# Retention, experts and a Fourier mixing block on one core: batch 0's stores and batch 1's loads ahead of the first layer, another order of conversions, folds, splits and rows

## The chip, the core and the metric

The kernel runs on one core of one Trainium2 chip. The metric is the device time of one execution in microseconds (us). The kernel before takes 799.32 us, the median of three runs (796.78, 799.32, 805.36).

## What is computed

Three blocks follow each other, on 4 batches of S = 576 rows of D = 512 numbers. The change lies in the third.

```python
x = attention(q, k, v)            # retention, 8 heads of 64
x = moe(x)                        # one of 8 experts for each row, F = 1024
X = np.real(np.fft.fft(np.fft.fft(x, axis=1), axis=2))
u = x + X
un = (u - mean(u)) / sqrt(var(u) + 1e-6)
return u + np.maximum(un @ w_ch1, 0) @ w_ch2     # 512 -> 2048 -> 512
```

## The kernel before

Products are made in 16-bit floats: each matrix is split into a high part (a scaled cast on ScalarE, L281) and a low part (what the cast lost, on VectorE, L286), and a product is three matrix products (high by high, high by low, low by high).

**The third block.** `channels` (L1577 and after) computes it. `tr` is the object that transforms a batch. Of one batch `load` (L1224) brings the rows in three tiles; `even` and `odd` (L1243, L1257) fold a tile on VectorE, with the tiles `fee` and `foo` as results, and `twice` (L1267) folds tiles 0 and 1 once more; `down` (L1279) multiplies the folded tiles by tables of cosines and sines, five groups to a batch; `take` copies a group's result out on ScalarE; `across` multiplies these by the second table, and `merge` adds the result to the rows; `sums` and `rate` make mean and rate of each row; `norm` writes the normalized rows as high and low part to the DRAM tensor `un`, and `keep` writes u to the DRAM tensor `u`. `steps(b)` is a generator that does all this for one batch in pieces.

**Batch 0.** Its 576 rows are transformed while TensorE ends the last expert. The rows of the first 512 then go through the first layer, in 16 steps f of 128 of the 2048 columns. `first(f, ...)` (L1651) issues the 12 products of 128 by 512 of a step; the first four steps are issued ahead of the loop. In the loop `for f in range(16)` ScalarE makes the relu (`gr`, L1852) and its cast (`hd`, L1853), and VectorE the low part of `hd` (L1854). Between these steps the loop calls generators, one piece at a time: `last` (the end of batch 0's norms and the stores `keep`), `rest` (splits of the first layer's pieces 4 to 7; conversion of pieces 6 and 7 of the second layer's matrix from 64-bit floats, `raw` to `wst`; their `absmax` on ScalarE; the peak over all pieces, with a product on TensorE, `peak`; `scale`, whose last instruction makes `ws`; the splits of pieces 6 and 7 and then of 0 to 5, two to a step), and from f = 7 on `tr.steps(1)` (batch 1's load, folds and transform).

**The second layer.** `for t in range(4)` makes the output of 128 rows in one pass over 16 rows of the matrix, one for each f: three products of 128 by 512 each (L1870), all added in one bank. Row f needs `hd` of step f, and the piece f // 2 of the second layer's matrix. Between the rows stand the rest of `tr.steps(1)` and pieces of `sums` (which add up blocks of the matrix, for the next loop). After the third pass `fetch(512)` asks for the next rows of `un`, transposed, in `gxt`. The loop over r0 = 512 and on takes 256 rows at a time and is the same in both kernels; j counts its turns.

**Useless products.** `still(n, ps)` (L1618) issues n products of 128 by 512 whose result nobody reads: STILL[0] = 8 ahead of batch 0's first `down`, STILL[1] = 22 in batch 1's first `down`, STILL[2] = 16 ahead of the first product of row 512.

**What sets the order.** Each engine works through its instructions in the order in which the program issues them; that order is the order of the calls. All loads and stores on SyncE (the DMA queue SPq) too go in the order of their calls. Pools set when a buffer comes free: three banks `g1` for the first layer, three buffers `gr`.

Of the kernel before, what the change touches and what calls it, by code (L numbers as in the profile page):

```python
# [20 lines left out]
E, FF = 8, 2048  # L21
# [22 lines left out]
EARLY_C1 = 2  # L44
LATE = 4
IDLE = 2, 2, 9, 7, 0
STILL = 8, 22, 16


PEAKS = 10, 14  # L50
# [2 lines left out]
DONE = 14  # L53
# [958 lines left out]
def moe(octx, tc, nc, A, xs, x2, rows_in, rows_out, pieces, weights, who, conv, low, start, beyond, z, padded, hid0, mt0, wst, small):  # L1012
# [126 lines left out]
    for e in range(E):  # L1139
        w, n = weights(e), CAPS[e] if e < E - 1 else HEAD  # L1140
        if e == E - 1:
            pieces.more = None
        xt, mt = X.pop(e)
        tiles = (n + 127) // 128

        todo = halves(weights, conv, 2 * e, 8, [("fetch", (fetch, e + 1))] if e + 1 < E else ()) if e else first
        hid = wk.tile([128, 2, 8, n], FP16, tag="hid", name="hid", padded_shape=[128, 2, 8, CAP])
        hid = [hid[:, x] for x in range(2)]
        for f in range(8):
            if e == 0 and f == 0:  # L1150
                four = [bank()[:, 0:n] for _ in range(4)]
                for part in (0, 2, 1):
                    for g in range(4):
                        products(nc, four[g], *w.dst, xt, f + g, (part,))
            if e == 0 and f < 4:
                ps = four[f]
            else:
                ps = bank()[:, 0:n]
                products(nc, ps, *w.dst, xt, f)
            for do in todo[f]:  # L1160
                do()
            if f == 4 and e + 2 < E:
                pad(e + 2)
            for _ in relu(nc, ps, hid, f):
                pass
        fs, fill = factors(w, mt, tiles + (end.n + 127) // 128, small) if e == E - 1 else factors(w, mt, tiles)
        if e == E - 1:
            end.fs = fs

        def sides(mt=mt, tiles=tiles, n=n, e=e):  # L1170
            for i, m in ((n // 128, n % 128), (tiles + end.n // 128, end.n % 128 if e == E - 1 else 0)):
                if m:

                    to, k = mt[:, i, 0:1], 128 // m
                    nc.vector.tensor_scalar(out=to, in0=to, scalar1=float(k), scalar2=side[k], op0=ALU.mult, op1=ALU.add)

        late = 0 < e < E - 1
        if not late:
            fill()
            sides()  # L1180
        if e == E - 1:
            mx.close()
            yield
        todo = halves(weights, conv, 2 * e + 1, tiles, [("factors", (f,)) for f in (fill, sides) if late]) if e else [[sizes]]
        for t in range(tiles):

            amid = partial(weights(e + 1).spread, 0, lambda: bank()[:, 0:128]) if e and t == 0 else None
            out(w, hid, mt, fs, t, n, todo[t], amid)
    end.hidden(range(LATE), bank)
    ctx.close()  # L1190
    yield end
# [12 lines left out]
class Transform:  # L1204
# [16 lines left out]
        nc.vector.memset(self.eps, 1e-6)  # L1221
        self.xy, self.ee, self.oo, self.z, self.st = {}, {}, {}, {}, {}

    def load(self, b, places=None):  # L1224

        nc, x2, r = self.nc, self.x2, b * S
        self.xy[b], self.ee[b], self.oo[b], self.z[b] = xy, ee, oo, z = places or self.own
        nc.gpsimd.memset(xy[0][0:1, 1, :], 0.0)
        nc.gpsimd.memset(xy[1][0:1, 1, :], 0.0)
        for t in range(3):  # L1230
            nc.gpsimd.memset(oo[t][:, 0:1], 0.0)
        for t, (k, n) in enumerate(TL):
            m = n if t < 2 else 2 * n
            i = nc.sync.dma_start(out=xy[t][:m, 0, :], in_=x2[r + k : r + k + m, :])
            if b < 2 and t == 0:
                self.rows.before(i)
            p = 1 if t < 2 else 0
            by_rows(nc, xy[t][p:n, 1, :], x2[r + k + n : r + k + 2 * n - p, :])
# [306 lines left out]
    def steps(self, b, wait=0):  # L1545

        self.load(b)
        yield
        for t in range(3):
            self.even(b, t)  # L1550
            if wait:
                yield
            self.odd(b, t)
            yield
        self.twice(b, 0)
        self.twice(b, 1)
        yield
        for _ in range(wait):
            yield
        for i in range(5):  # L1560
            self.take(b, i, self.down(b, i))
            yield
        for t in range(3):
            if t:
                self.sums(b, t - 1)
            self.merge(b, t, *self.across(b, t))
            yield
        self.sums(b, 2)
        yield
        yield from self.end(b)  # L1570


def channels(ctx, tc, nc, A, w1, w2, un, u, out, tr, wst, idn, late, jobs):
# [17 lines left out]
    def fetch(r):  # L1591
        X[r] = xt = room().rearrange("p (k n) -> p k n", k=8)
        nc.sync.dma_start_transpose(out=xt, in_=un[r : r + 256, :])  # L1593
# [11 lines left out]
        q, tag = ((p1, "g1"), (tr.ps, "z"), (tr.ps, "z"), (tr.ps, "z"), (p1, "g1"), (p1, "g1"), (p2, "g2"), (p2, "g2"))[turn[0] % 8]  # L1605
        return q.tile([128, 512], FP32, tag=tag, name="bank")

    late.hidden(range(LATE, 8), bank)
    tr.root()
    tr.turn(idn)  # L1610
    for j in range(EARLY_C1, 4):
# [10 lines left out]

    tr.still = still
    still(STILL[0], z[0])
    tr.even(0, 0)
    leave()
    tr.even(0, 1)
    tr.twice(0, 0)
# [57 lines left out]
    turns = {i: tr.turned(0, i, norms[i], xt, bank()) for i in (0, 3)}  # L1686
    weave(adds[2])
    leave()
    next(turns[0])
    next(turns[3])  # L1690
    next(rates[1])
# [16 lines left out]
    for f in range(4):  # L1708
        first(f, place(f, 1), half[1])

    def last():

        tr.norm(0, 2, 2)
        tr.sums(0, 2)
        yield
        weave(tr.rate(0, [2]))
        tr.norm(0, 5)
        yield
        for i in range(6):
            tr.keep(0, i)  # L1720
        yield

    def convert(j):

        V = nc.vector
        t = w2.pieces[j] = wst.tile([128, 1024], FP32, tag="wst", name="wst")
        for i in range(2):
            raw = wst.tile([128, 512, 2], I32, tag="wst", name="raw")
            nc.sync.dma_start(out=raw, in_=jobs[8 + j][0][:, i])
            convert_first(V, raw, t[:, 512 * i : 512 * i + 512].bitcast(I32))  # L1730
            yield
            convert_second(V, raw, t[:, 512 * i : 512 * i + 512].bitcast(I32))
            yield
        w2.absmax(j)

    def rest():

        for j in range(4, 8):
            w1.split(j)
            yield  # L1740
        done = DONE - 8
        for j in range(done, 8):
            yield from convert(j)
        for j in range(done, 8):
            nc.sync.dma_start(out=jobs[8 + j][1], in_=w2.pieces[j])
        w2.peak(0)
        for j in range(2):
            w2.load(j)
        yield
        w2.spread(0)  # L1750
        w2.scale(0)
        for j in range(done, 8):
            w2.split(j)
        yield
        for j in range(2, done):
            w2.load(j)
        for j in range(done):
            w2.split(j)
            if j % 2:
                yield  # L1760


    def blocks(k):
# [21 lines left out]
    def sums():  # L1785
# [31 lines left out]
    TWICE = 1, 4  # L1817
    WAIT = 1
    LEFT = 6
    T_SLOTS = [(t, f) for t in range(0, 4) for f in (4, 12)]  # L1820

    def old(r, n):

# [12 lines left out]
        )  # L1836


    more, left, hid, end = tr.steps(1), rest(), [], last()
    for f in range(16):  # L1840
        if f < 4:
            ps = ahead[f]
        else:
            ps = p1.tile([128, 512], FP32, tag="g1", name="g1")
            first(f, ps, xt)
        if f >= 7:
            next(more, None)
        next(end, None)
        next(left, None)
        r = wk.tile([128, 512], FP32, tag="gr", name="gr")  # L1850
        hd = hp.tile([128, 2, 512], FP16, tag="hd", name="hd")
# [11 lines left out]
        V.tensor_scalar(out=fs[:, j : j + 1], in0=fs[:, 0:1], scalar1=c, scalar2=None, op0=ALU.mult)  # L1863
    us = [old(256 * a, 256) for a in range(2)]
    left = sums()
    for t in range(4):
        ps = p2.tile([128, 512], FP32, tag="g2", name="g2")
        for f in range(16):
            for i, (m, x) in enumerate(((h2, 0), (h2, 1), (l2, 0))):
                nc.tensor.matmul(  # L1870
                    out=ps,
                    lhsT=hid[f][:, x, 128 * t : 128 * t + 128],
                    rhs=m[:, f // 2, 512 * (f % 2) : 512 * (f % 2) + 512],
                    start=(f == 0 and i == 0),
                    stop=(f == 15 and i == 2),
                )
            if f == 7 or (t, f) == (0, 3):
                next(more, None)
            if (t, f) in T_SLOTS:
                next(left, None)  # L1880
        next(more, None)
        if t == 2:
            for _ in more:
                pass
            fetch(512)
# [478 lines left out]
```

## Time and profile before

| | us |
|---|---|
| median of three runs | 799.32 |
| the profiled execution | 797.81 |
| its span in the trace | 796.0 |
| TensorE busy in it | 736.8 (93%) |
| VectorE busy in it | 591.1 (74%) |
| ScalarE busy in it | 411.5 (52%) |

The profile is of one execution. PE is TensorE, DVE VectorE, ACT ScalarE, SP SyncE; times count from the span's start. A busy share over the whole span is a mean over stages with different limits, so the stages are read one by one. PEclk is the granted clock of TensorE as a share of full speed: 1.00 is 2.4 GHz, 0.50 is 1.2 GHz. A line of a timeline has the start, the time until the end of the last of its instructions, the engine, the line of the kernel, what it writes and reads, and in brackets how long the engine was idle before it, and what released it.

### The profile page before, as it was taken

How to read it: one execution, taken by the hardware profiler on the slowest of the kernel's cores; microseconds unless marked ns; L12 is line 12 of the kernel's file. 1: busy time of each engine (PE TensorE's matmuls, PEld its weight loads, DVE VectorE, ACT ScalarE, POOL GpSimd, SP SyncE). 2: the span in 40 equal slices, each digit the busy share in tenths (PEclk: the TensorE clock that was granted, in tenths of full speed). 3: DMA queues.
4: the chain of work that ended last, by engine and by line, in shares of the span. 5: the costliest groups of instructions: out<-in, count | busy, mean ns of one | idle time of the engine just before them, and what ended most of it. 6: DMA issues, size and time to landing. Idle time of an engine off the chain costs nothing. (4 is left out here: it accounts for less than half of the span.)

```text
span 796.0 us, 17230 instructions
## 1 busy us (share of the span) xinstructions
PE 736.8 (93%) x6571; PEld 549.3 (69%) x6571; DVE 591.1 (74%) x1432; ACT 411.5 (52%) x829; POOL 128.6 (16%) x225
## 2 busy tenths in 40 slices
PE   8888797999999989889989999899899999999996
PEld 5677684646556646557644547778788888888885
DVE  3678887599888987867796976968867595736462
ACT  1356656479798887845827544416432361414140
POOL 3566443002201220113000011010010101010101
PEclk9999999999999998999998999999999999999998
DMA  9998349999999999950538257610370016110000
GB/s 296 360 301 298 130 130 303 322 284 379 273 341 327 271 309 330 254 181 29 168 95 314 96 185 200 181 54 2 123 192 2 27 61 168 52 53 3 28 1 27
DMA packets 91930, 142.29 MB, mean 179 GB/s; under 512 B 48116, under 2 KB 49017, under 8 KB 90814
## 3 DMA queue, kind: packets, MB, share of 16 engines
q1 hardware_dynamic: 87246, 126.78, 50.5%
q0 software_dynamic: 4592, 14.31, 5.0%
q8 instruction: 54, 0.88, 0.4%
q14 instruction: 38, 0.31, 0.1%
HBM read 97.55 MB, written 35.12 MB: 167 GB/s over the span
## 5 line engine op out<-in xcount | busy, mean ns | idle before, releaser
L1656 PE MATMUL g<-gxt,wh 128*128 128x256 f16 (+1 forms) x992 | 143.3, 284 | 2.4 <-DMA gxt<-un 2.4
L1970 PEld LDWEIGHTS <-hd 128*128 128x128 f16 x1176 | 115.1, 98 | 26.3 <-issue 6.0
L1656 PEld LDWEIGHTS <-wh 128*128 128x128 f16 x1056 | 103.2, 98 | 28.3 <-issue 7.1
L286 DVE SCALAR_TENSOR_TENSOR wl<-wst,ws,wh 128x1024 f16<-128x1024 f32 (+1 forms) x82 | 100.4, 1253 | 9.6 <-ACT wh L281 9.4
L281 ACT ACTIVATE wh<-wst,ws 128x1024 f16<-128x1024 f32 x80 | 89.2, 1141 | 29.2 <-DVE ws L274 29.2
L815 PE MATMUL ps<-xt,wh 128*128 128x320 f16 (+4 forms) x544 | 80.1, 287 | 13.0 <-DMA xt<-xs 7.9
L845 PE MATMUL ps<-wh,hid 128*128 128x512 f16 (+2 forms) x528 | 84.5, 302 | 0.2 <-ACT hid L831 0.2
L815 PEld LDWEIGHTS <-wh 128*128 128x128 f16 x640 | 58.0, 101 | 38.0 <-issue 19.8
L1830 POOL DMA_INDIRECT out<-u,orow x18 | 19.3, 1075 | 389.7 <-DVE u L1999 291.3
L1970 PE MATMUL g<-wh,hd 128*128 128x256 f16 x448 | 78.3, 273 | 2.5 <-DVE s L1941 1.6
L1656 PE MATMUL g<-gxt,wl 128*128 128x256 f16 (+1 forms) x496 | 80.4, 285 | 0.0
L845 PEld LDWEIGHTS <-hid 128*128 128x128 f16 (+2 forms) x792 | 46.4, 100 | 42.3 <-issue 2.7
L1941 DVE SCALAR_TENSOR_TENSOR s<-g,r 128x256 f32<-128x256 f32 x168 | 53.1, 371 | 29.6 <-ACT hd L1935 28.9
L239 ACT ACTIVATE wh<-wst 128x1024 bf16<-128x1024 f32 x66 | 69.3, 1051 | 4.9 <-DVE wst L311 3.8
L1999 DVE SCALAR_TENSOR_TENSOR u<-g,ffs,u 128x256 f32<-128x256 f32 (+1 forms) x63 | 34.1, 567 | 49.3 <-PE g L1970 48.7
L1934 ACT ACTIVATE r<-g 128x256 f32<-128x256 f32 x56 | 21.1, 378 | 90.9 <-PE g L1656 84.9
L1970 PE MATMUL g<-e,hd 128*128 128x256 f16 x504 | 61.6, 277 | 5.5 <-DVE u L1999 4.5
L1914 ACT ACTIVATE hd<-s 128x640 f16<-128x640 f32 x56 | 41.3, 737 | 47.1 <-DVE s L1941 47.0
L859 POOL DMA_INDIRECT x<-y,mt x25 | 32.1, 1285 | 194.7 <-ACT y L857 156.3
L1970 PE MATMUL g<-wl,hd 128*128 128x256 f16 x224 | 61.0, 272 | 0.0
L1656 PEld LDWEIGHTS <-wl 128*128 128x128 f16 x528 | 51.9, 98 | 11.7 <-issue 1.1
L845 PE MATMUL ps<-wl,hid 128*128 128x512 f16 (+2 forms) x264 | 56.3, 301 | 0.0
(302 smaller groups left out, 1292.5 us busy)
## 6 DMA issues: line engine op xcount, KB each, us to landing
wst<-in_moe_w SPq DMA_DIRECT2D x64, 512.0 KB
raw<-in_ch SPq DMA_DIRECT2D x14, 1024.0 KB
qk<-in_qkv SPq DMA_DIRECT2D x18, 512.0 KB
vk<-in_qkv SPq DMA_DIRECT2D x16, 512.0 KB
pair<-ch SPq DMA_DIRECT2D x32, 256.0 KB
ch<-d SPq DMA_DIRECT2D x14, 512.0 KB
wst<-ch SPq DMA_DIRECT2D x14, 512.0 KB
u<-u SPq DMA_DIRECT2D x9, 512.0 KB
```

The lines of the kernel that those rows point to most:

```text
L239: self.nc.scalar.activation(out=x, in_=t, func=ACTF.Abs, accum_out=self.am[:, j : j + 1])
L281: self.nc.scalar.activation(out=self.dst[0][:, j, :], in_=self.pieces[j], func=ACTF.Copy, scale=self.by(j))
L286: self.nc.vector.scalar_tensor_tensor(out=l[:, j, c], in0=self.pieces[j][:, c], scalar=self.by(j), in1=h[:, j, c], op0=ALU.mult, op1=ALU.s ...
L815: nc.tensor.matmul(out=ps, lhsT=m[:, k, 128 * f : 128 * f + 128], rhs=xt[:, x + k, :], start=(k == 0 and i == 0), stop=(k == 3 and i == last),
L845: nc.tensor.matmul(out=ps[r * j : r * j + r, 0:d], lhsT=hid[x][:, f, 128 * t : 128 * t + r], rhs=m[:, 4 + f // 2, c : c + d], start=(f == ...
L859: nc.gpsimd.indirect_dma_start(out=x2[:, :].rearrange("t (k d) -> (t k) d", k=k), out_offset=bass.IndirectOffsetOnAxis(ap=mt, axis=0), in_ ...
L1656: nc.tensor.matmul(out=ps, lhsT=m[:, k + 4 * (f // 8), 128 * (f % 8) : 128 * (f % 8) + 128], rhs=xt[x][:, k, :], start=(k == 0 and i == 0) ...
L1914: nc.scalar.activation(out=hd[:, 0, 2:7], in_=s, func=ACTF.Copy, scale=C2 / 2)
L1934: nc.scalar.activation(out=r, in_=p[:, 1:3], func=ACTF.Relu)
L1941: V.scalar_tensor_tensor(out=d, in0=x, scalar=0.0, in1=y, op0=ALU.max, op1=op)
L1970: nc.tensor.matmul(out=ps, lhsT=hid[k][:, y, x, :], rhs=E[w][m][k], start=(k == 0 and m == y == 0), stop=(k == 7 and y == 1),)
L1999: V.scalar_tensor_tensor(out=y, in0=p, scalar=fs[:, c : c + 1], in1=y, op0=ALU.mult, op1=ALU.add)
```

## The change

1. STILL becomes 0, 0, 4.
2. In the last expert, the last two splits of its list are issued after the last output tile and no more inside it.
3. Batch 0's first fold is issued among the last expert's tiles.
4. Batch 0's stores `keep` of tiles 0 and 1, the loads of piece 6 (`begin(6)`) and of batch 1's tiles 0 and 1 are issued ahead of the first layer.
5. One generator `beside` takes the place of `rest` and `last`: batch 1's folds (f2, f6, f7, f8) come ahead of the conversions (f9 to f12), the peak is at f13, the scale and the splits of pieces 6 and 7 at f14, the splits of pieces 0 to 5 at f15, all six in one step.
6. Batch 1's transform (`across_rows`) starts at f = 10 with one `down` a step; the rest of it and the pieces of `sums` have new places in the second layer (MORE, T_SLOTS), and `fetch(512)` comes after the fourth row of the third pass.
7. The second layer takes its rows in the order 12 to 15, 0 to 11.

```diff
-STILL = 8, 22, 16
+STILL = 0, 0, 4
...
-            out(w, hid, mt, fs, t, n, todo[t], amid)
+            do = todo[t] if e < E - 1 else todo[t][:-1]
+            out(w, hid, mt, fs, t, n, do, amid)
+        if e == E - 1:
+            todo[-1][-1]()
...
-    late.hidden(range(LATE, 8), bank)
+    late.hidden(range(LATE, LATE + 1), bank)
+    tr.even(0, 0)
+    late.hidden(range(LATE + 1, 8), bank)
...
     still(STILL[0], z[0])
-    tr.even(0, 0)
     leave()
...
+    for i in (0, 3, 1, 4):
+        tr.keep(0, i)
...
+    begin(DONE - 8)
...
+    tr.load(1, (0, 1))
...
+    def beside():
+        done = DONE - 8
...
         tr.norm(0, 2, 2)
         tr.sums(0, 2)
+        w1.split(4)
         yield
         weave(tr.rate(0, [2]))
         tr.norm(0, 5)
+        for i in (2, 5):
             tr.keep(0, i)
+        tr.load(1, (2,))
+        yield
+        tr.even(1, 0)
+        w1.high(5)
+        tr.odd(1, 0)
+        yield
+        w1.low(5)
+        yield
+        w1.split(6)
+        begin(7)
+        yield
+        w1.split(7)
+        yield
+        tr.even(1, 1)
+        tr.odd(1, 1)
+        yield
+        tr.even(1, 2)
+        tr.odd(1, 2)
+        yield
+        tr.twice(1, 0)
+        tr.twice(1, 1)
+        yield
         for j in range(done, 8):
+            for _ in convert(j):
+                yield
+        for j in range(2):
+            w2.load(j)
         for j in range(done, 8):
             nc.sync.dma_start(out=jobs[8 + j][1], in_=w2.pieces[j])
         w2.peak(0)
-        for j in range(2):
-            w2.load(j)
         yield
         w2.spread(0)
         w2.scale(0)
...
         for j in range(done):
             w2.split(j)
-            if j % 2:
-                yield
...
+    DOWNS = 10
+    MORE = [(0, 3), (0, 7), (0, 15), (1, 3), (1, 7), (1, 9), (1, 11), (1, 13), (1, 15), (2, 1), (2, 3)]
+    T_SLOTS = [(1, 14), (2, 6), (2, 9), (2, 12), (2, 15), (3, 3), (3, 8), (3, 13)]
+    ROWS = *range(12, 16), *range(12)
...
-        if f >= 7:
+        next(left, None)
+        if f >= DOWNS:
             next(more, None)
-        next(end, None)
-        next(left, None)
...
-        for f in range(16):
+        for at, f in enumerate(ROWS):
...
-                    start=(f == 0 and i == 0),
-                    stop=(f == 15 and i == 2),
+                    start=(at == 0 and i == 0),
+                    stop=(at == 15 and i == 2),
```

The order of ScalarE's instructions at the end of the first layer, before. L281 are the highs of the second layer's splits; the last `gr` and `hd` are those of f = 15, the two ahead of them of f = 14.

```order
L1852 ACTIVATE gr_7291<-g1_7260 128x512
L1853 CAST hd_7292<-gr_7291 128x512
L1306 COPY fz3_6316<-zps_7309 128x256
L1306 COPY fz3_6316<-zps_7309 128x34
L281 ACTIVATE wh1_77<-wst_7279,ws_7213 128x1024
L281 ACTIVATE wh1_77<-wst_7281,ws_7213 128x1024
L1852 ACTIVATE gr_7319<-g1_7296 128x512
L1853 CAST hd_7320<-gr_7319 128x512
L281 ACTIVATE wh1_77<-wst_7283,ws_7213 128x1024
L281 ACTIVATE wh1_77<-wst_7285,ws_7213 128x1024
```

The same place in the change (L1890 and L1891 are the relu and the cast; the first row is f = 14's cast):

```order
L1891 CAST hd_7262<-gr_7261 128x512
L281 ACTIVATE wh1_77<-wst_7208,ws_7217 128x1024
L281 ACTIVATE wh1_77<-wst_7210,ws_7217 128x1024
L281 ACTIVATE wh1_77<-wst_7279,ws_7217 128x1024
L281 ACTIVATE wh1_77<-wst_7281,ws_7217 128x1024
L281 ACTIVATE wh1_77<-wst_7283,ws_7217 128x1024
L281 ACTIVATE wh1_77<-wst_7285,ws_7217 128x1024
L1457 COPY bs_7315<-zps_7299 128x256
L1458 COPY sm_7313<-zps_7300 128x1
L1459 COPY df_7314<-zps_7300 128x1
L1890 ACTIVATE gr_7327<-g1_7266 128x512
L1891 CAST hd_7328<-gr_7327 128x512
```

Six highs and three copies of batch 1's merge now stand between the cast of f = 14 and the relu of f = 15; before, two highs stood there and two copies.

VectorE's order around the end of the first layer's step f = 15, in the change: the last of the six lows (L286), batch 1's first merge, and the low part of f = 15's `hd` (`hd_7328`).

```order
L286 SCALAR_TENSOR_TENSOR wl1_78<-wst_7285,ws_7217,wh1_77 128x1024
L1441 MEMSET mv_7307 128x6
L1442 MEMSET sq_7308 128x6
L1460 TENSOR_TENSOR sm_7313<-zps_7300,bs_7315 128x256
L1461 TENSOR_TENSOR df_7314<-zps_7300,bs_7315 128x256
L1464 TENSOR_TENSOR fxy0_6302<-fxy0_6302,sm_7313 128x257
L1465 TENSOR_TENSOR fxy0_6302<-fxy0_6302,df_7314 128x255
L1464 TENSOR_TENSOR fxy0_6302<-fxy0_6302,df_7314 128x257
L1465 TENSOR_TENSOR fxy0_6302<-fxy0_6302,sm_7313 128x255
L1466 BN_STATS st_7306<-fxy0_6302 128x6
L1467 BN_AGGR mv_7307<-st_7306 128x2
L1892 TENSOR_TENSOR hd_7328<-gr_7327,hd_7328 128x512
```

Before, the merge stood behind all `hd`, and two lows stood between one `hd` and the next.

TensorE's order at the start of the second layer, before (the last group of `down`, then rows f = 0 and 1; `hd_6894` is f = 0's):

```order
L1291 MATMUL zps_7309<-f_sn_1971,foo2_6311 128x290
L1870 LDWEIGHTS hd_6894
L1870 MATMUL g2_7335<-wh1_77,hd_6894 128x512
L1870 LDWEIGHTS hd_6894
L1870 MATMUL g2_7335<-wh1_77,hd_6894 128x512
L1870 LDWEIGHTS hd_6894
L1870 MATMUL g2_7335<-wl1_78,hd_6894 128x512
```

And in the change, the end of the third row and the fourth (`hd_7328` is f = 15's):

```order
L1909 MATMUL g2_7351<-wl1_78,hd_7262 128x512
L1909 LDWEIGHTS hd_7328
L1909 MATMUL g2_7351<-wh1_77,hd_7328 128x512
L1909 LDWEIGHTS hd_7328
L1909 MATMUL g2_7351<-wh1_77,hd_7328 128x512
L1909 LDWEIGHTS hd_7328
L1909 MATMUL g2_7351<-wl1_78,hd_7328 128x512
```

The `hd` made last is now read in the fourth row of the first pass, and was read in its last.

## Rows read from the trace of the kernel before

**Rows 1.** Busy time by stretch (columns in the first row), granted clock PEclk

```profile
core 0: us, PE busy (x) PEld busy (x) DVE busy (x) ACT busy (x) POOL busy (x), PEclk, DMA share, GB/s
340.00:360.00 20.00, 16.17 (x129) 10.74 (x128) 12.73 (x38) 8.06 (x19) 3.48 (x9) 1.00 0.56 184
...
385.00:406.00 21.00, 21.00 (x101) 9.63 (x99) 17.71 (x32) 15.82 (x26) 0.00 (x0) 1.00 0.78 244
...
416.17:423.00 6.83, 6.32 (x16) 3.13 (x17) 4.83 (x12) 2.61 (x6) 0.00 (x0) 0.50 0.44 147
...
500.00:525.00 25.00, 21.25 (x176) 17.67 (x174) 24.24 (x64) 8.43 (x19) 0.00 (x0) 0.93 0.56 154
...
518.57:522.00 3.43, 3.43 (x19) 2.45 (x17) 3.29 (x10) 0.27 (x1) 0.00 (x0) 0.50 0.42 143
```

**Rows 2.** Timeline of TensorE: waits and useless products (L1621)

```profile
342.97 0.37 PE L815 MATMUL ps<-xt,wh 128*128 128x160 f16 x3 [2.88 <-PEq L2128]
...
353.97 1.89 PE L1621 MATMUL bank<-wh 128*128 128x512 f16 x8
...
408.71 4.91 PE L1621 MATMUL zps<-wh 128*128 128x512 f16 x22
416.68 2.30 PE L1291 MATMUL zps<-f_cs,fee 128*128 128x145 f32 x6 [3.06 <-DVE fee L1270]
418.77 1.91 PE L1656 MATMUL g<-gxt,wh 128*128 128x512 f16 x4
...
518.34 4.45 PE L1970 MATMUL g<-e,hd 128*128 128x256 f16 x24 [2.71 <-DVE u L1999]
```

**Rows 3.** Timeline of VectorE: the first fold of batch 0's tiles 0 and 1

```profile
349.56 0.68 DVE L1247 TENSOR_TENSOR xe<-fxy 128x512 f32<-128x512 f32 x1
...
351.15 0.68 DVE L1247 TENSOR_TENSOR xe<-fxy 128x512 f32<-128x512 f32 x1
```

**Rows 4.** Timeline of VectorE: conversions, peak, scale, splits

```profile
394.74 0.43 DVE L299 TENSOR_SCALAR wst<-raw 128x512 int32<-128x512 int32 x1 [1.65 <-DMA raw<-in_ch]
...
419.12 0.69 DVE L1854 TENSOR_TENSOR hd<-gr,hd 128x512 f16<-128x512 f32 x1
420.55 0.16 DVE L255 TENSOR_REDUCE wm<-am 128x1 f32<-128x8 f32 x1 [0.74 <-ACT wh L239]
...
425.21 0.16 DVE L274 RECIPROCAL ws<-wi 128x1 f32<-128x1 f32 x1
...
433.74 2.48 DVE L286 SCALAR_TENSOR_TENSOR wl<-wst,ws,wh 128x1024 f16<-128x1024 f32 x2 [0.49 <-ACT wh L281]
```

**Rows 5.** Timeline of ScalarE: copy, absmax, relu, cast, highs

```profile
419.01 0.46 ACT L1306 COPY fz<-zps 128x256 f32<-128x256 f32 x2 [10.15 <-PE zps L1291]
419.36 1.07 ACT L239 ACTIVATE wh<-wst 128x1024 bf16<-128x1024 f32 x1
...
420.41 0.60 ACT L1852 ACTIVATE gr<-g 128x512 f32<-128x512 f32 x1
421.04 0.62 ACT L1853 CAST hd<-gr 128x512 f16<-128x512 f32 x1
...
425.41 2.19 ACT L281 ACTIVATE wh<-wst,ws 128x1024 f16<-128x1024 f32 x2 [0.31 <-DVE ws L274]
```

**Rows 6.** Timeline of VectorE: first and last instruction of a merge of batch 1

```profile
440.77 0.41 DVE L1456 TENSOR_TENSOR sm<-zps,bs 128x256 f32<-128x256 f32 x1
...
443.61 0.18 DVE L1463 BATCH_NORM_AGGREGATE mv<-st 128x2 f32<-128x6 f32 x1
```

**Rows 7.** Timeline of TensorE: second layer, and the next rows

```profile
444.46 0.61 PE L1320 MATMUL zps<-f_sd,fz 128*128 128x128 f32 x4
...
452.07 0.60 PE L1870 MATMUL g<-wh,hd 128*128 128x512 f16 x2
...
477.98 3.62 PE L1621 MATMUL g<-wh 128*128 128x512 f16 x16
482.96 0.60 PE L1656 MATMUL g<-gxt,wh 128*128 128x256 f16 x4 [1.36 <-DMA gxt<-un]
```

More of the change, by code (lines that the diff above doesn't have):

```diff
@@ L1222, in __init__, with load @@
         self.xy, self.ee, self.oo, self.z, self.st = {}, {}, {}, {}, {}
-    def load(self, b, places=None):
+    def load(self, b, tiles=range(3)):
         nc, x2, r = self.nc, self.x2, b * S
[L1227 to L1230, printed above, removed]
+        self.xy[b], self.ee[b], self.oo[b], self.z[b] = xy, ee, oo, z = self.own
+        for t in tiles:
+            if t < 2:
+                nc.gpsimd.memset(xy[t][0:1, 1, :], 0.0)
             nc.gpsimd.memset(oo[t][:, 0:1], 0.0)
-        for t, (k, n) in enumerate(TL):
+        for t in tiles:
+            k, n = TL[t]
             m = n if t < 2 else 2 * n
@@ L1559, in steps, with across_rows @@
             yield
+        yield from self.across_rows(b)
+    def across_rows(self, b):
         for i in range(5):
@@ L1688, in channels, with begin @@
     leave()
+    for i in (0, 3, 1, 4):
+        tr.keep(0, i)
+    pieces = {}
+    def begin(j):
+        t = w2.pieces[j] = wst.tile([128, 1024], FP32, tag="wst", name="wst")
+        pieces[j] = t, [wst.tile([128, 512, 2], I32, tag="wst", name="raw") for _ in range(2)]
+        for i, raw in enumerate(pieces[j][1]):
+            nc.sync.dma_start(out=raw, in_=jobs[8 + j][0][:, i])
+    begin(DONE - 8)
     next(turns[0])
@@ L1709, in channels, with convert @@
         first(f, place(f, 1), half[1])
-    def last():
+    tr.load(1, (0, 1))
+    def convert(j):
+        t, raws = pieces[j]
+        for i, raw in enumerate(raws):
+            convert_first(V, raw, t[:, 512 * i : 512 * i + 512].bitcast(I32))
+            convert_second(V, raw, t[:, 512 * i : 512 * i + 512].bitcast(I32))
+            if i:
+                w2.absmax(j)
+            yield
+    def beside():
+        done = DONE - 8
+        ready = [f for j in range(done, 8) for f in (j, j)]
         tr.norm(0, 2, 2)
         tr.sums(0, 2)
+        w1.split(4)
         yield
@@ L1717, in last @@
         tr.norm(0, 5)
+        for i in (2, 5):
+            tr.keep(0, i)
+        tr.load(1, (2,))
         yield
-        for i in range(6):
-            tr.keep(0, i)
+        tr.even(1, 0)
+        w1.high(5)
+        tr.odd(1, 0)
         yield
[L1723 to L1730, printed above, removed]
-            yield
[L1732 to L1741, printed above, removed]
+        w1.low(5)
[14 more added lines that the diff above has]
+        yield
         for j in range(done, 8):
-            yield from convert(j)
+            for _ in convert(j):
+                yield
+        for j in range(2):
+            w2.load(j)
         for j in range(done, 8):
@@ L1758, in rest @@
             w2.split(j)
-            if j % 2:
-                yield
     def blocks(k):
@@ L1819, in channels @@
     LEFT = 6
-    T_SLOTS = [(t, f) for t in range(0, 4) for f in (4, 12)]
+    DOWNS = 10
+    MORE = [(0, 3), (0, 7), (0, 15), (1, 3), (1, 7), (1, 9), (1, 11), (1, 13), (1, 15), (2, 1), (2, 3)]
+    T_SLOTS = [(1, 14), (2, 6), (2, 9), (2, 12), (2, 15), (3, 3), (3, 8), (3, 13)]
+    ROWS = *range(12, 16), *range(12)
     def old(r, n):
@@ L1836, in store @@
         )
-    more, left, hid, end = tr.steps(1), rest(), [], last()
+    more, left, hid = tr.across_rows(1), beside(), []
     for f in range(16):
@@ L1865, in channels @@
     left = sums()
+    next(left)
     for t in range(4):
         ps = p2.tile([128, 512], FP32, tag="g2", name="g2")
-        for f in range(16):
+        for at, f in enumerate(ROWS):
             for i, (m, x) in enumerate(((h2, 0), (h2, 1), (l2, 0))):
@@ L1873, in channels @@
                     rhs=m[:, f // 2, 512 * (f % 2) : 512 * (f % 2) + 512],
-                    start=(f == 0 and i == 0),
-                    stop=(f == 15 and i == 2),
+                    start=(at == 0 and i == 0),
+                    stop=(at == 15 and i == 2),
                 )
-            if f == 7 or (t, f) == (0, 3):
+            if (t, at) in MORE:
                 next(more, None)
-            if (t, f) in T_SLOTS:
-                next(left, None)
[L1881 to L1885, printed above, removed]
+            if (t, at) == MORE[-1]:
+                for _ in more:
+                    pass
+                fetch(512)
+            if (t, at) in T_SLOTS:
+                next(left, None)
         o = us[t // 2][:, t % 2]
```

## The prediction

> **What bounds the kernel now.** I read the table of stretches first. Over the first layer of the rows 0 to 511 (385 to 406 us) TensorE has no gap, and VectorE is busy 17.71 of 21 us; in the first pair of rows after them (500 to 525 us) VectorE is busy 24.24 of 25 us and TensorE only 21.25 [rows 1]. TensorE is therefore the engine to follow, with VectorE close behind it. The timeline of TensorE then shows where it does nothing useful. Eight useless products run at 353.97, ahead of batch 0's transform. Twenty-two run from 408.71 and last 4.91 us; after them the engine still waits 3.06 us for batch 1's folds, until 416.68 [rows 2]. Sixteen run from 477.98, and a wait of 1.36 us for the transposed rows comes behind them, until 482.96 [rows 7]. The clock is the third thing. From 416.17 to 423.00 it is granted at 0.50 (1.2 GHz of 2.4), and again from 518.57 to 522.00 [rows 1]; the idle times just before are 3.06 and 2.71 us [rows 2]. Those stretches cost about half of their busy time, 6.32 and 3.43 us [rows 1]: 3.2 and 1.7 us.
>
> **Part by part.**
>
> *Batch 0's folds.* The eight products are 1.7 us (353.97 to 355.69) [rows 2]. The first fold runs on VectorE from 349.56 to 351.15, behind the last `hidl`, and the next tile's from 351.15 [rows 3]. Earlier by one fold (1.6 us) at most, the second fold is then limited by the landing of its tile. I take 0.95 us, with ends of 0.4 and 1.7 us. The moved output tile (y's copy and scatter before the last two splits) is what gives an earlier load; it is inside these ends. The gain ends in VectorE's queue below.
>
> *The f loop.* On VectorE the same instructions stand up to the end of the last conversion, but for one more `hd` (0.6 us). Before, VectorE has 21 − 17.71 = 3.3 us without work in 385 to 406, of which 1.65 us is the wait for `raw` [rows 1, 4]. The change asks for these doubles and for batch 1's rows ahead of the first layer, so I take 2.9 of these 3.3 us away. What comes instead is in the ScalarE order: `absmax` of piece 6 stands ahead of f10's relu, so that `hd` 10 on VectorE waits for absmax 1.05 (419.36 to 420.41), a copy of 0.46, the relu 0.63 and the cast 0.62, together 2.8 us [rows 5]. From 419.2, where the conversions end before (419.12 and the rows' spacing) [rows 4]: 419.2 − 0.95 − 2.9 + 0.6 + 2.8 = 418.8. Nothing is gained there within 0.6 us, and I leave the scale at 425.2, where `ws` is made [rows 4]: piece 7's absmax, the same chain of 2.8 us, then the peak on TensorE. The folds are ready for batch 1's first `down` product, since they now end at f8, two steps ahead of it; the 4.91 + 3.06 us on TensorE go, and so does the stretch at half clock. But TensorE only runs ahead of VectorE by this: it has done f13 by about 418.7 and then stands until the peak at 423.5, some 4.8 us, a wait that is new.
>
> *The second layer's first pass.* Here the rows' order rests on one piece, and it decides my sign. In the order of ScalarE the six highs of pieces 0 to 5 stand behind f14's cast and ahead of f15's relu; before, only two stood there. On VectorE the six lows and batch 1's first merge stand ahead of the last `hd`. ScalarE: from the scale, two highs 2.19 (425.2 to 427.4), the copy 0.46, relu and cast 1.2: 429.05; six highs at 1.09: 435.6; three small copies put at 0.6, relu and cast 1.2: 437.4 [rows 5]. VectorE: the lows, 1.24 each (2.48 for two) [rows 4], end at about 437.6; the merge takes 3.0 us (440.77 to 443.79) [rows 6]; so 440.65, and with the `hd` 0.6 us 441.25. TensorE needs that `hd` now in its fourth row (12, 13, 14, then 15) and not in its last: it has done three rows by 431.2 and stands until 437.4 for one product and until 441.25 for the others. At 441.25 the kernel before had five rows of its first pass left (it ends at 444.46) [rows 7]; the changed one has 12.7. Rows cost (477.98 − 452.07) / 40 = 0.648 us [rows 7], and the merges' products between the rows are still ahead in both. It is behind by 7.7 × 0.648 = 5.0 us.
>
> *The end of the four passes.* 477.98 + 5.0 = 483.0. The transposed rows are asked for three rows into the third pass, and the 4.98 us before the next layer (477.98 to 482.96) [rows 7] shrink to 4 useless products, 0.86 us. First product of row 512: 483.85, which is 0.9 us later than before.
>
> *The clock.* The new waits (4.8 us from 418.7, and 10 us from 431.2) are longer than the two that brought the clock to 0.50. From the two cases of before, 1.7 to 3.2 us are lost after the long wait [rows 1]; I take 2.5. After the shorter one first(14) loses 0.5 to 2.4 us, and ScalarE's chain to f15 starts behind it; I take 0.9. Below zero this can't go, since the clock is at 1.00 in the cases it is compared with. Sum: 0.9 + 2.5 + 0.9 = +4.3 us; with the ends 0.9 and 0.9 + 3.2 + 2.4 = 6.5.
>
> From 483 on the order is the same. VectorE binds the first pair of rows [rows 1], so a backlog of sums there would show; there are as many of them done by then as before, and VectorE has spare time in the 33 us before. I take 0, with −1 to +2. The other queue to look at is SyncE's: the stores of u and the loads of batch 1 and of piece 6 now go ahead of two stores of un that wait for norms, tile 2's load behind them; its fold is six steps later. I take nothing.
>
> The profiled execution is 797.81 us, 796.0 of them span; the median of the three runs is 799.32. 797.81 + 4.3 = 802.1, or 803.6 on the median's scale; I say 803.
>
> *A rule against this change.* The rows first: TensorE was idle 2.88 us up to 342.97, and the clock stayed at 1.00 between 340 and 360; after 3.06 us it fell [rows 1, 2]. The Trainium skill ("TensorE: Matmul & The Clock Gate", Part 1: The HAM clock gate) says that throttled is the default state and that activity releases it, so products of no use are worth their time where the engine would stand. By that rule each place where they go could cost a half-clock stretch; by the rows only the two long waits do. It is the third rival below.
>
> **Rivals.**
>
> (1) *The last `hd` is not late.* If the scale were ready some 10 us sooner, or the last `hd` went ahead of the splits, TensorE would go on at 431.2: 10 us less and no half-clock behind it, 0.9 − 10 = −9 us: 788.7, or 790 on the median's scale. Each us by which `ws` is earlier is one us of it. For it: VectorE's rows have gaps that I have to guess, and TensorE has 8 us fewer to do before the peak. Against it: both orders put the splits ahead, and VectorE has no gap left to give.
>
> (2) *It waits, and the clock holds or half of the hold goes.* 0 to −5 us, 795 to 800: the same within 1%.
>
> (3) *Slower: the clock stays at 0.50 from 421 on until after the hold.* Price: first(14), 12 products of 512 columns at 0.43 instead of 0.215 (four take 1.91 at 418.77 and not 1.03) [rows 2], is 2.6 us later, its `down` 0.6 more, both in the chain to f15; after the hold 3.2; one stretch of 1.7 in batch 0's transform, where eight products went. 0.9 + 3.2 + 3.2 + 1.7 = +9.0 us, 808 on the median's scale. It decides from the point where the clock doesn't come back between the two waits. For it: the clock fell for 6.83 us after a wait a third as long [rows 1]. Against it: the second case lasted half as long.
>
> **How the numbers follow.** A measurement of this kernel can tell about 1% (8 us) from no change. My forecast, +0.9 to +6.5 us, has 0.50; (2) has 0.10; (1) has 0.18; (3) has 0.22. Of (1) nearly all is faster by over 1% (791.3 and below), and (3) lies about the upper bound of 807.3, mostly above, as does a little of the forecast. So 0.18 faster, 0.60 same, 0.22 slower. The range goes from 789 (most of rival 1) to 809 (most of rival 3); the forecast's own is 800 to 806.
>
> **What would show it.** Right: no useless products at 350 and 405, `ws` at 424 to 427; ScalarE's six highs in one run; one wait of TensorE of 6 us or more for the cast and the last `hd` in the first pass; half clock behind it; no wait for the transposed rows at 480. Wrong: rows of the second layer without a gap at the fourth, or a first product of row 512 before 478. If the folds are still late, TensorE waits for `fee` at f10.

## The result and the profile after

The changed kernel takes 805.13 us (median of 20 runs, 801.09 to 809.44), the kernel before 798.83 us (20 runs). The ratio is 1.0069, with a 95% interval of 1.0049 to 1.009: slower by some 5.5 us (0.69%). The forecast was 803 us, within 1%, range 789 to 809. The profiled execution of the changed kernel has a span of 800.2 us, 4.2 more than before.

The stretches of the changed kernel (columns as in [rows 1]; granted clock third from the end):

```profile
core 0: us, PE busy (x) PEld busy (x) DVE busy (x) ACT busy (x) POOL busy (x), PEclk, DMA share, GB/s
...
385.00:406.00 21.00, 21.00 (x103) 10.12 (x101) 19.76 (x44) 14.24 (x22) 0.00 (x0) 1.00 0.36 120
...
418.00:424.00 6.00, 1.98 (x10) 0.78 (x8) 3.16 (x7) 2.93 (x9) 0.00 (x0) 1.00 0.37 119
424.00:432.00 8.00, 6.97 (x21) 3.60 (x21) 6.00 (x12) 6.59 (x11) 0.00 (x0) 0.57 0.82 301
432.00:442.00 10.00, 3.50 (x21) 1.86 (x19) 9.93 (x17) 7.46 (x14) 0.00 (x0) 0.82 0.49 159
442.00:450.00 8.00, 7.84 (x39) 5.14 (x40) 3.96 (x14) 2.59 (x10) 0.00 (x0) 0.80 0.00 0
```

TensorE's timeline in the kernel before has these lines beside those of [rows 2] and [rows 7]:

```profile
335.55 0.22 PE L265 MATMUL ps<-diag,onesb 128*128 128x128 bf16 x1
...
355.69 2.95 PE L1291 MATMUL bank<-f_cs,fee 128*128 128x145 f32 x18
...
385.31 1.03 PE L1656 MATMUL g<-gxt,wh 128*128 128x512 f16 x4
...
445.57 0.60 PE L1870 MATMUL g<-wh,hd 128*128 128x512 f16 x2
```

TensorE's timeline in the changed kernel (L2166 is the branch to the overflow code, which TensorE jumps over here, L1909 the second layer, L1631 a useless product):

```profile
334.16 0.22 PE L265 MATMUL ps<-diag,onesb 128*128 128x128 bf16 x1
...
342.98 0.69 PE L815 MATMUL ps<-xt,wl 128*128 128x160 f16 x4 [3.25 <-PEq L2166]
...
355.85 2.95 PE L1295 MATMUL bank<-f_cs,fee 128*128 128x145 f32 x18
...
385.63 1.03 PE L1665 MATMUL g<-gxt,wh 128*128 128x512 f16 x4
...
413.65 1.02 PE L1665 MATMUL g<-gxt,wh 128*128 128x512 f16 x4 [1.72 <-ACT gr L1890]
...
425.03 0.26 PE L265 MATMUL peak<-diag,onesb 128*128 128x128 bf16 x1 [5.05 <-DVE diag L260]
...
427.13 1.91 PE L1665 MATMUL g<-gxt,wh 128*128 128x512 f16 x4
...
434.73 0.38 PE L1909 MATMUL g<-wl,hd 128*128 128x512 f16 x1
438.01 0.39 PE L1909 MATMUL g<-wh,hd 128*128 128x512 f16 x1 [2.90 <-ACT hd L1891]
442.16 0.61 PE L1909 MATMUL g<-wh,hd 128*128 128x512 f16 x1 [3.76 <-DVE hd L1892]
...
442.98 1.06 PE L1324 MATMUL zps<-f_sd,fz 128*128 128x128 f32 x4
...
445.12 0.62 PE L1909 MATMUL g<-wh,hd 128*128 128x512 f16 x2
...
485.32 1.03 PE L1631 MATMUL g<-wh 128*128 128x512 f16 x4
486.19 0.60 PE L1665 MATMUL g<-gxt,wh 128*128 128x256 f16 x4
```

The wait for the folds (3.06 us, [rows 2]) and the one for the transposed rows (1.36 us, [rows 7]) are gone. In their place stand 1.72 us for a bank, 5.05 us for the peak, and 2.90 + 3.76 us at the fourth row of the second layer, for the cast and then the low part of the last `hd`; these two are called the hold below. ScalarE's timeline of the changed kernel, from the second absmax to the last relu and cast; the six highs stand ahead of these:

```profile
421.04 1.06 ACT L239 ACTIVATE wh<-wst 128x1024 bf16<-128x1024 f32 x1 [5.27 <-DVE wst L311]
...
430.11 6.34 ACT L281 ACTIVATE wh<-wst,ws 128x1024 f16<-128x1024 f32 x6
...
436.71 0.59 ACT L1890 ACTIVATE gr<-g 128x512 f32<-128x512 f32 x1
437.34 0.62 ACT L1891 CAST hd<-gr 128x512 f16<-128x512 f32 x1
```

And VectorE's: the first fold of batch 0's tiles 0 and 1 (before in [rows 3]), two `hd` that wait for an absmax ahead of their relu, `ws`, the six lows, the last `hd`:

```profile
347.67 0.68 DVE L1251 TENSOR_TENSOR xe<-fxy 128x512 f32<-128x512 f32 x1
...
351.44 0.68 DVE L1251 TENSOR_TENSOR xe<-fxy 128x512 f32<-128x512 f32 x1
...
414.28 0.69 DVE L1892 TENSOR_TENSOR hd<-gr,hd 128x512 f16<-128x512 f32 x1 [2.71 <-ACT hd L1891]
...
423.70 0.69 DVE L1892 TENSOR_TENSOR hd<-gr,hd 128x512 f16<-128x512 f32 x1 [2.70 <-ACT hd L1891]
...
426.32 0.16 DVE L274 RECIPROCAL ws<-wi 128x1 f32<-128x1 f32 x1
...
431.28 7.26 DVE L286 SCALAR_TENSOR_TENSOR wl<-wst,ws,wh 128x1024 f16<-128x1024 f32 x6 [0.36 <-ACT wh L281]
...
441.44 0.66 DVE L1892 TENSOR_TENSOR hd<-gr,hd 128x512 f16<-128x512 f32 x1
```

Where the time went shows best between marks of TensorE's timeline: S, the product that spreads the last expert's peak (L265); T, batch 0's first `down` product; F, the first product of f4; R, the first product of row 512; E, the first product with an e block. Times in us, one profiled execution each; the ratio is to the kernel before, from all timed runs.

| kernel | S to T | T to F | F to R | R to E | E to end | ratio (95%) |
|---|---|---|---|---|---|---|
| before | 20.14 | 29.62 | 97.65 | 23.99 | 289.05 | 1 |
| changed | 21.69 | 29.78 | 100.56 | 23.99 | 290.02 | 1.0069 (1.0049 to 1.009) |
| e1_natural | 22.83 | 29.78 | 94.18 | 24.30 | 291.04 | 0.9992 (0.9966 to 1.0019) |
| e2_hd_first | 22.81 | 29.79 | 93.41 | 25.68 | 290.39 | 0.9984 (0.996 to 1.0009) |
| e3_fill | 22.62 | 29.78 | 100.35 | 23.99 | 289.30 | 1.0048 (1.0011 to 1.0085) |
| e4_absmax | 21.43 | 29.77 | 96.51 | 23.99 | 291.63 | 1.0019 (0.9981 to 1.0057) |
| e5_nat_abs | 23.06 | 29.79 | 89.89 | 23.99 | 289.78 | 0.9923 (0.9892 to 0.9953) |
| e6_before_still | 18.68 | 34.15 | 97.43 | 25.32 | 289.78 | 0.9994 (0.9956 to 1.0031) |
| e7_after_still | 23.68 | 28.90 | 104.29 | 23.99 | 290.11 | 1.0118 (1.0061 to 1.0175) |
| e8_nat_out | 19.55 | 31.28 | 94.17 | 23.99 | 291.03 | 0.9965 (0.9927 to 1.0004) |
| e9_before_out | 24.48 | 29.62 | 96.96 | 23.99 | 290.21 | 1.0049 (1.0022 to 1.0077) |
| e10_nat_abs_out | 19.29 | 31.02 | 89.86 | 23.98 | 291.97 | 0.991 (0.9877 to 0.9943) |
| e11_with_8 | 21.57 | 28.89 | 89.85 | 23.99 | 289.69 | 0.9902 (0.9872 to 0.9933) |

In these profiles the change loses 2.9 us from F to R, 1.7 us from S to F and 1.0 us behind E; ahead of S, where both kernels have the same instructions, its execution happens to be 1.4 us shorter (334.16 against 335.55), so that the spans differ by 4.2. The last column of stages scatters by 2.9 us over all these kernels, whose instructions there are the same, so nothing is read from that 1.0 either.

### The profile page after: what moved, and what is told of

Same layout as the page of the kernel before. It is cut to its first block, busy times and chain, and to the rows that moved or that the text cites. A ratio compares the mean times of both kernels' runs of the same rounds, so it can differ in the third digit from the quotient of the medians.

```text
span 800.2 us, 17151 instructions
## 1 busy us (share of the span) xinstructions
PE 729.7 (91%) x6529; PEld 547.7 (68%) x6529; DVE 592.3 (74%) x1432; ACT 411.6 (51%) x829; POOL 127.9 (16%) x225
## 5 line engine op out<-in xcount | busy, mean ns | idle before, releaser
L286 DVE SCALAR_TENSOR_TENSOR wl<-wst,ws,wh 128x1024 f16<-128x1024 f32 (+1 forms) x82 | 100.2, 1251 | 9.2 <-ACT wh L281 9.2
L281 ACT ACTIVATE wh<-wst,ws 128x1024 f16<-128x1024 f32 x80 | 89.1, 1140 | 26.7 <-DVE ws L274 26.3
L815 PE MATMUL ps<-xt,wh 128*128 128x320 f16 (+4 forms) x544 | 78.4, 281 | 8.7 <-DMA xt<-xs 5.6
L2008 PE MATMUL g<-e,hd 128*128 128x256 f16 x504 | 59.9, 273 | 5.0 <-DVE u L2037 4.0
```

What stands on the lines that cost most here:

```text
L281: self.nc.scalar.activation(out=self.dst[0][:, j, :], in_=self.pieces[j], func=ACTF.Copy, scale=self.by(j))
L286: self.nc.vector.scalar_tensor_tensor(out=l[:, j, c], in0=self.pieces[j][:, c], scalar=self.by(j), in1=h[:, j, c], op0=ALU.mult, op1=ALU.s ...
L815: nc.tensor.matmul(out=ps, lhsT=m[:, k, 128 * f : 128 * f + 128], rhs=xt[:, x + k, :], start=(k == 0 and i == 0), stop=(k == 3 and i == last),
L2008: nc.tensor.matmul(out=ps, lhsT=hid[k][:, y, x, :], rhs=E[w][m][k], start=(k == 0 and m == y == 0), stop=(k == 7 and y == 1),)
```

## The experiments

**e1_natural: the rows in their old order.**

```diff
-    ROWS = *range(12, 16), *range(12)
+    ROWS = (*range(16),)
```

> The changed kernel with the second layer's rows in their old order, 0 to 15. Theory A (the last hd, 15th, is what TensorE waits for in its fourth row): the waits of 2.9 and 3.8 us at the fourth row go, the first pass ends some 8 us sooner, and the first product of row 512 comes at about 478 instead of 486.2; the span is 6 to 8 us shorter (792 to 794), faster than before by about 0.5%. Theory B (the clock at half speed is what costs, not the wait): 2 us at most. Theory C (VectorE binds the pair of rows after it, so that what TensorE gains is waited for there): the first product at 478 all the same, but the waits for u behind it grow by as much, and the span stays within 2 us of 800.

F to R falls from 100.56 to 94.18, by 6.4 us, and the ratio from 1.0069 to 0.9992. The waits at the fourth row are gone. Of the waits left in the first pass of TensorE's timeline the two longest are for ScalarE's copies between the rows, 1.37 and 1.03 us; one of 0.36 us is for a split:

```profile
437.03 0.49 PE L1331 MATMUL zps<-f_cd,fz 128*128 128x128 f32 x2 [1.37 <-ACT bs L1457]
...
442.14 0.41 PE L1331 MATMUL zps<-f_cd,fz 128*34 128x128 f32 x2 [1.03 <-ACT bs L1457]
...
479.19 1.03 PE L1631 MATMUL g<-wh 128*128 128x512 f16 x4
```

A holds; B is far too small. R to E grows by 0.3 us only, so C falls here.

**e2_hd_first: the six splits behind the last `hd`; the rows in the new order.**

```diff
         for j in range(2, done):
             w2.load(j)
+        yield
         for j in range(done):
             w2.split(j)
```

> The changed kernel with the six splits of pieces 0 to 5 issued behind the last hd and no more ahead of it; the rows stay in the new order. A: the last hd is made at about 437 instead of 442.0, rows 0 and on follow the splits with no long wait; the first pass ends 5 to 6 us sooner, first product of row 512 at about 481, span 795. B: 2 us at most. C: first product at 481, span within 2 us of 800.

F to R is 93.41, ratio 0.9984. In TensorE's timeline the same row now waits 1.80 us in place of 2.90 + 3.76:

```profile
437.65 0.39 PE L1910 MATMUL g<-wh,hd 128*128 128x512 f16 x1 [1.80 <-DVE hd L1893]
```

Two edits of different kinds, on the row that reads and on the `hd` that is read, take away the same loss. It is the pair of both in the change that costs. Here R to E does grow, by 1.7 us, in three waits of 0.54 to 0.55 us for VectorE's `s`: C is a part of this one.

**e3_fill: useless products in the new waits.**

```diff
+        still(20, p2.tile([128, 512], FP32, tag="g2", name="fill"))
         w2.spread(0)
...
             for i, (m, x) in enumerate(((h2, 0), (h2, 1), (l2, 0))):
+                if (t, at, i) in ((0, 3, 0), (0, 3, 1)):
+                    still(14 + 2 * i, p2.tile([128, 512], FP32, tag="g2", name="fill"))
```

> The changed kernel with useless products in its new waits: 20 ahead of the peak, 14 and 16 about the first product of the fourth row. The waits themselves stay. A: the clock is at 1.00 from 420 to 450, and the pass ends 1.5 us sooner (the half-clock time after 442.2 is 3.1 us), no more, since the half-clock time after the peak lies in the wait for the last hd: span 798 to 799. B: 4 us or more, span 796 or less. If the useless products themselves are late they cost up to 0.5 us each place.

F to R is 100.35, 0.2 us less, and the ratio's interval overlaps that of the changed kernel. With the 20 products ahead of the peak the clock is granted at 1.00 from 420 to 440, and the half-clock stretch behind the peak (424 to 432 above) is gone. The last `hd` is ready 56.5 us behind F all the same (443.84 − 387.36), so that stretch costs nothing. In the hold the run falls short of what was expected of it: the clock is at 0.57 from 440 to 444, and the last 16 products are late. They end at 445.28, after 5.30 us instead of the 3.44 that they would take at 0.215 us each, 1.4 us behind the last `hd`. The timeline of TensorE has the two groups in the hold:

```profile
433.70 3.19 PE L1631 MATMUL fill<-wh 128*128 128x512 f16 x14
...
439.98 5.30 PE L1631 MATMUL fill<-wh 128*128 128x512 f16 x16
```

So what the half clock behind the hold costs can't be read from this run; the trace of the changed kernel puts it at 1.4 us (below). The run gives no support to B.

**e4_absmax: each absmax one step later, and e5_nat_abs: that and the old row order.**

```diff
-            if i:
-                w2.absmax(j)
             yield
...
             for _ in convert(j):
                 yield
+            w2.absmax(j)
```

> The changed kernel with each absmax of pieces 6 and 7 issued one step later, so that it stands behind the relu and cast of f10 and f12 on ScalarE and VectorE does not wait for these. The two waits of VectorE (2.71 and 2.70 us) go. A: conversions end at 418 instead of 420.9, ws at 421 instead of 426.4, the last hd at 437 instead of 442.0; first product of row 512 some 5 us sooner; span 795. B: 2 us at most. C: first product at 481, span within 2 us of 800.

> The rows in their old order and both absmax one step later, together. From the first product of f4 to the first of row 512 the kernel before takes 97.7 us, the changed one 100.6, old row order alone 94.2, absmax alone 96.5. A (each wait of the chain through the scale and the first pass is worth its length): about 90, and the time is 3 to 4 us under that of the old row order alone: ratio 0.994 to 0.996. C (VectorE binds the pair of rows after 512): the 90 us come, but the time from the first product of row 512 to the first of the e blocks grows from 24.0 to 27 or more, and the ratio stays at 0.998 to 1.000.

VectorE's two waits of 2.7 us are gone in e4; its timeline has `ws` here:

```profile
423.97 0.16 DVE L274 RECIPROCAL ws<-wi 128x1 f32<-128x1 f32 x1
```

That is 36.4 us behind F (423.97 − 387.57) instead of 40.7 (426.32 − 385.63), and F to R falls by 4.05 us; in e5 by 10.7, nearly the sum of 6.4 and 4.05. The chain through the scale costs its length, with either order of the rows. In the timed runs e4 alone is not clear of the changed kernel (1.0019 against 1.0069, the intervals overlap); e5 is clear of e1. The ratio of e5 is even below what was expected, 0.9923, and R to E is 23.99: C falls.

**e6_before_still and e7_after_still: the useless products alone.**

```diff
-STILL = 8, 22, 16
+STILL = 0, 0, 4
```

(e6, in the kernel before; e7 is the reverse in the changed one.)

> The kernel before with 0, 0 and 4 useless products in place of 8, 22 and 16; nothing else. A: the 22 stood in a wait for the folds that ends at the same time without them, and most of the 16 in the wait for the transposed rows; the 8 are up to 1.7 us: -1.5 to +1 us, ratio 0.998 to 1.001. The Trainium skill's rule (TensorE: Matmul & The Clock Gate, Part 1: The HAM clock gate), that activity releases the clock: two more stretches at half clock, +3 to +5 us, ratio 1.004 to 1.006. Beside it the place ahead of batch 0's transform is a second look at the wait at the branch (2.88 us in the kernel before, 3.25 to 3.94 in the five with the change): 2.9 if the change makes it longer, 3.3 or more if it varies by itself.

> The changed kernel with the old 8, 22 and 16 useless products. A: 12 more ahead of row 512 cost 12 x 0.215 = 2.6 us there, the 8 up to 1.7 us, the 22 nothing, since TensorE waits 1.7 and 5.1 us for VectorE just behind them: +2.6 to +4.3 us, ratio 1.010 to 1.012. By the skill's rule they give back clock: 0 to -2 us, ratio 1.004 to 1.007.

In e6 the ratio is 0.9994, as A had it, but the profile shows effects of opposite sign and not one of none. S to T is 1.5 us shorter, and T to F 4.5 us longer: TensorE waits 1.02 us for a fold at 357.29, and the clock goes to 0.50 in the transform behind it. Its stretches there:

```profile
358.12:361.12 3.00, 2.75 (x13) 1.54 (x9) 2.79 (x9) 1.38 (x6) 0.00 (x0) 0.77 0.49 132
361.12:364.12 3.00, 3.00 (x10) 2.42 (x10) 2.16 (x4) 0.50 (x3) 0.00 (x0) 0.50 0.25 101
364.12:367.12 3.00, 3.00 (x18) 3.00 (x18) 0.00 (x0) 0.42 (x2) 0.00 (x0) 0.59 0.02 5
```

From F to R the 22 and the 12 are worth nothing (97.43 against 97.65), although TensorE then stands 7.80 us for the folds and 2.68 for the rows. But R to E grows by 1.3 us: behind the wait for the rows the clock falls once more, where it stayed at 1.00 in the kernel before (TensorE's timeline, and a stretch with columns as in [rows 1]):

```profile
486.70 1.01 PE L1656 MATMUL g<-gxt,wh 128*128 128x256 f16 x4 [2.68 <-DMA gxt<-un]
...
486.00:490.00 4.00, 3.30 (x19) 2.45 (x19) 0.00 (x0) 0.00 (x0) 0.48 (x4) 0.57 0.95 321
```

In these two places the rule of the Trainium skill (TensorE: Matmul & The Clock Gate, Part 1: The HAM clock gate), that activity releases the clock, has a case. The profiled execution is one of the slower of its ten (803.55 us, median 800.97). In all ten the mean granted clock is 0.980 on average, and 0.985 in the 25 of the kernel before, yet the time is the same (0.9956 to 1.0031): as far as these runs can tell, the products cost about as much time as they give back.

In the changed kernel the products cost 3.7 us from F to R. Of these 2.6 are the 12 at row 512; the other 1.1 us are clock, which is at 0.50 for 5.3 us behind the last `hd` (447.7 to 453.0) where it was for some 3. The half-clock stretch behind the peak is gone in e7, to no gain: the last `hd` comes 56.5 us behind F here too. The ratio is 1.0118 (four runs; its interval still overlaps that of the changed kernel).

**e8_nat_out and e9_before_out: the last expert's last two splits.** e8 is e1 with them back inside the last output tile; e9 is the kernel before with nothing changed but that move.

```diff
-            do = todo[t] if e < E - 1 else todo[t][:-1]
-            out(w, hid, mt, fs, t, n, do, amid)
-        if e == E - 1:
-            todo[-1][-1]()
+            out(w, hid, mt, fs, t, n, todo[t], amid)
```

> The rows in their old order and the last expert's last two splits again inside its last output tile, as before the change. From the last expert's spread to batch 0's first down product the kernel before takes 20.1 us, the five with the change 21.4 to 22.8, and the clock falls to half in all five at the end of the wait at the branch. D (the moved splits bring TensorE to the branch sooner and make that wait longer): the wait is 2.9 us, the clock stays, 20.1 us come back, and the time is 2 us under the old row order alone: ratio 0.996 to 0.997. E (the wait varies or another part does it): 21.4 or more, ratio 0.998 to 1.000.

> The kernel before with the last expert's last two splits moved behind its last output tile, the one part of the change ahead of the third block; nothing else. D (this move makes the wait at the branch longer and so brings the half clock): the wait is 3.3 us or more, a stretch at half clock follows, and from the last expert's spread to the first product of f4 it takes 51 to 53 us where the kernel before took 49.8; ratio 1.001 to 1.004. E (the wait has another cause): 2.9 to 3.0 us, no half clock, 49 to 50 us; ratio 0.998 to 1.000.

e9 is slower by 0.49% (0.22 to 0.77): S to F takes 54.10 us instead of 49.76. In e8 S to F is 50.83 against 52.61 in e1. In the kernel before the move costs time, as D says; in the changed one the profile says so too, but the timed runs of e8 and e1 (0.9965 and 0.9992) are not clear of each other. TensorE's timeline in e9 at the branch and behind it:

```profile
346.62 0.44 PE L815 MATMUL ps<-xt,wl 128*128 128x160 f16 x4 [3.40 <-PEq L2131]
...
349.73 0.45 PE L815 MATMUL bank<-xt,wl 128*128 128x160 f16 x2 [1.66 <-issue]
```

And e9's stretches of 3 us there, with the clock falling to 0.50 (columns as in [rows 1]):

```profile
345.00:348.00 3.00, 1.22 (x14) 0.98 (x14) 0.85 (x4) 0.30 (x1) 0.00 (x0) 1.00 0.16 23
348.00:351.00 3.00, 1.34 (x11) 1.28 (x11) 0.04 (x2) 0.25 (x1) 0.00 (x0) 0.55 0.88 284
351.00:354.00 3.00, 3.00 (x25) 3.00 (x24) 0.65 (x2) 0.41 (x3) 0.00 (x0) 0.50 0.83 268
```

The wait at the branch is 2.88 us in the kernel before and 2.97 in e6, which is the same up to there; the clock stays at 1.00 behind both. With the splits moved it is 3.25 to 3.94 (eight profiles), and with them back in the changed kernel 3.27, 3.03 and 3.49 (e8, e10, e11); the clock falls behind all eleven. What tells the two groups apart is how long it stays at 0.50: 6.8 us or more in the eight, 3.4 us in e8, e10 and e11. The eight have a second gap, of 0.81 to 2.25 us, that ends some three us behind the wait; e8, e10 and e11 have none, and the kernel before and e6, with 0.75 and 0.92 us there, don't lose the clock. Of D the mechanism is only half borne out: between e8, e10 and e11, which are the same up to there, the wait varies by half a us, and why it is longer with the change stays open.

**e10_nat_abs_out and e11_with_8: the parts that pay, together.** e10 is e5 with e8's edit; e11 has STILL = 8, 0, 4 besides.

> The rows in their old order, both absmax one step later, and the last expert's splits where they were before the change. The first two gave a ratio of 0.9923 together. If the gains add: the place of the splits another 1 to 2.7 us, ratio 0.989 to 0.991. If they don't: 0.992 to 0.994.

> The same with the 8 useless products ahead of batch 0's first down product put back. If they keep the clock up in batch 0's transform, as the kernel before with and without them let it look (29.6 us from the first down product to f4 with them, 34.2 without): 29 to 30 us there, clock 1.00, and up to 2 us less in all, ratio 0.988 to 0.990. If they are only time: 1.7 us more at most from the spread to f4, ratio 0.991 to 0.993.

Ratios 0.991 and 0.9902, medians 792.29 and 792.26 us, under both kernels. The gain of e10 over e5 (0.991 against 0.9923) is inside their intervals. The eight products shorten T to F by 2.1 us and lengthen S to T by 2.3: no gain in sum. The clock is not what they change here. In batch 0's transform it is at 1.00 without them too, as e10's stretches show:

```profile
354.00:357.00 3.00, 2.19 (x12) 0.75 (x10) 2.79 (x9) 1.04 (x5) 1.07 (x2) 1.00 0.25 96
357.00:360.00 3.00, 2.71 (x14) 2.11 (x15) 2.93 (x7) 0.80 (x4) 0.00 (x0) 1.00 0.57 172
```

and the mean clock of the timed runs is 0.986 in both. The products stand in the place of waits for the folds, 0.65, 0.26 and 0.17 us in e10 and none in e11.

## Why the prediction was right

The sign, the size and the place held: the last `hd`, behind six splits and a merge, is read too early, and the gain of the f loop is spent there. e1 and e2 show this from both sides (6.4 and 7.2 us from F to R). The steps, one by one:

- *Batch 0's folds*: wrong. Forecast 0.95 us earlier (0.4 to 1.7), measured 1.7 us later at F. The step gave the moved output tile as the source of an earlier load and put it inside these ends; e9 shows that it costs, alone 4.3 us in its profile and 0.49% in time. The first fold does start 0.5 us earlier, counted from S (347.67 − 334.16 against 349.56 − 335.55), but the second starts 1.7 us later (351.44 − 334.16 against 351.15 − 335.55), behind the last `hidl` of the last expert, whose products run at half clock in the changed kernel (342.8 to 349.6). What I left out is the wait at the branch: at 2.88 us in [rows 2] it was already longer than the 2.71 us behind which the clock fell at 518.
- *The f loop*: right. The conversions end at 421.0 and `ws` at 426.3; from F that is 0.8 us later than before, where I had it 0.95 later (the same time with an earlier F). VectorE waits 2.71 and 2.70 us where 2.8 was forecast, TensorE 5.05 at the peak where 4.8 was; e4 and e5 show that these waits cost 4.1 to 4.3 us. Inside this step two terms were off and cancel: VectorE's time without work in 385 to 406 fell by 2.05 us (17.71 us busy before, 19.76 after) and not by 2.9, and the conversions end 35.4 us behind F and not 34.4; from there to `ws` it takes 5.3 us and not 6.4.
- *The first pass*: right in mechanism, its start off. The last `hd` is ready at 442.1, 56.5 us behind F (forecast 441.25 − 384.36 = 56.9). The wait is 6.7 us and not 10, as the step f15 ran at half clock, so that the three rows before it began at 433.0.
- *The clock*: too high. The 0.9 us for the first wait cost nothing, since ScalarE's six highs and not TensorE set the last `hd`. Behind the long wait the products of the merge take 2.14 us (442.98 to 445.12) instead of 1.11 ([rows 7] shows their start), and two products 0.8 instead of 0.4: 1.4 us, where 2.5 was forecast. The rows of `un` are asked for after the fourth row of the third pass and not after three; no wait for them is left, so nothing hangs on it.
- *In sum* from F to R: forecast 4.3 + 0.95 = 5.25 us, measured 2.9; the 2.3 us between are, rounded, 0.4 in the last `hd` and 0.9 and 1.1 in the clock. So the first step was too low by 2.7 us and the others too high by 2.3. The mechanism of the first pass was right; that the total came within a few us was in part luck.
- *The first pair of rows* after 512: 23.99 us in both, as forecast.

Of the rivals, the first is what e1 and e2 make of the kernel: without the hold F to R is 6.4 and 7.2 us shorter, where the rival counted 10 for it, and against the kernel before it is 3.5 to 4.2 us shorter and not 9, with no difference in the timed runs (0.9992 and 0.9984). The second, a hold by half or without half clock, didn't come: the hold is 6.7 us and the clock is at 0.50 behind it. The third didn't come as a whole, since the clock was back at 1.00 when the three rows ran; the half-clock stretch that it counted for batch 0's transform came ahead of it, at the branch.

## What to carry to other kernels

A consumer's order and a producer's order have to be read together: when rows are taken in the order in which their weights come, look up where the other operand of each row stands in its engine's queue, and what else stands ahead of it there. An instruction that waits (here an absmax for the conversion) should stand behind those that don't, on an engine that works in order. Useless products on an engine that waits for another one are worth little either way, and a profile of one execution can mislead on them: taking them out of the kernel before shortened one stage, let the clock fall in two others, and left the time as it was (e6). Where the engine would not have waited they cost their own time (the 12 at row 512 in e7). Follow the engine that sets the wait.

## What the runs showed of the hardware beyond that

The clock fell after waits of 3.03 us and more at the branch and not after 2.97 or 2.88. Elsewhere it fell behind shorter ones: 2.71 us at 518 in the kernel before, 2.68 us at row 512 in e6, and 1.02 us in e6 in a transform of short products; behind 0.65 us in the same transform in e10 it stayed. The length of one wait alone did not tell which.
